# First pair's q and k turned on TensorE, q's second order made by a copy on VectorE

## Chip, core and metric

One core of a Trainium2 chip runs the kernel. Time is device microseconds of one execution, and lower is better. A run's time is given as the median of three. Besides that there is one profiled execution, whose trace is read here.

## What is computed

Attention comes first, then two layers that mix each token's features. `q`, `k` and `v` are float32, (4, 8, 1152, 64): 4 batches, 8 heads, 1152 positions, 64 features. The weights lie in memory as 8-byte floats, which the kernel reads as pairs of 32-bit words.

```python
q_pool = q.reshape(B, H, S // 2, 2, D).mean(axis=3)
scores = (1 / np.sqrt(D)) * np.matmul(q_pool, k.transpose(0, 1, 3, 2))
attn = exp(scores - max) / (sum + 1e-09)
x = np.matmul(attn, v)                 # heads side by side: (2304, 512)
h = x @ w_in1
x = (h * np.cos(h)) @ w_out1
h = x @ w_in2
out = (h / (1 + np.exp(-h))) @ w_out2  # (2304, 512)
```

## The kernel before

**Numbers in two halves.** TensorE multiplies float16 operands here. So that float32 accuracy is kept, each operand is scaled by a power of two and split into a high float16 half and a low one (`hi`, `lo`: the rest after rounding). A product then takes several matmuls: high by high, high by low, low by high.

**Pairs.** The 32 heads of attention are worked through in 16 pairs: pair j of batch b holds heads j and j + 4. A pair has 9 query tiles of 128 rows (576 pooled queries per head, four tiles each, and one tile that holds the remaining 64 of both). Batches follow each other, four pairs each.

**Preparation of a pair** is `pair_prep` (L453 to L514), on data that `pair_loads` (L429) fetched. All loads are issued by SP, whose queue also issues every other DMA of the program, in one order. GpSimd adds q's neighbouring rows (L456); VectorE takes absolute maxima of k, q and v (L126); a small matmul and three small VectorE operations make scale factors (`scale_steps`). Then come the splits. For k and v, `split` (L445) writes the high half by ScalarE and the low half by VectorE. For q two orders are wanted: `qn[:, 0]` holds high then low in its 2 x 64 columns, `qn[:, 1]` low then high. ScalarE writes the high half twice (L491), VectorE makes the low half (L492) and copies it into the second order (L495). One DMA transpose on SP's queue turns both orders of q, 18 blocks of 128 x 128, into `qT` (L497), and a second one turns k's 18 blocks into `kT` (L507).

**A tile** (`tile_scores`, `tile_exp`, `tile_hi`, `tile_lo`, `tile_pv`). TensorE multiplies both orders of a q block with k (L531, L539): the first order gives high by high and low by low, the second the cross terms. VectorE scales the scores out of PSUM into `sc` and keeps the extreme (L550), in a part of 512 and one of 640 columns; each part has one PSUM buffer, so that the next tile's scores wait until VectorE has emptied it. ScalarE takes the exponential (L558) and the high half (L564), GpSimd the low half (L569), a DMA transpose turns both (`hlT`, L571), and TensorE multiplies by v (`pv`, L582, L586). Four buffers each hold `sc`, `hl` and `hlT`, and the product with v follows four tiles behind.

**Beside the tiles** run, a step at a time, the preparation of the next pair and the loads of the one after it, in the first batch the preparation of the first layer's weights (16 pieces; ScalarE L201 and L202, VectorE L203, L207, L211), and from the second batch on the first layer itself (`g1_unit` L667, `g2_unit1` L722 on TensorE, the cosine on VectorE and ScalarE L695 to L711). The second layer and its product of halves (L836) make the tail.

**Who sets the order.** The code is written as generators that take turns; each engine's final order is made by a scheduler when the program is built, from priorities (`early`, `ahead`) and its own notion of durations. `pin` (L123) keeps the marked instructions in the order in which they are written. On the chip each engine runs its list strictly in order, and waits where an operand is missing.

Of the kernel before, what the change touches and what calls it, by code (L numbers as in the profile page):

```python
# [11 lines left out]
F32 = mybir.dt.float32  # L12
# [15 lines left out]
NB_N, NB_SC, NB_H, NB_T, NB_S = 2, 4, 4, 4, 5  # L28
# [20 lines left out]
def attention_moe_moe_kernel(ctx, tc, q, k, v, w_in1, w_out1, w_in2, w_out2, out):  # L49
# [3 lines left out]
    nc = tc.nc  # L53
# [20 lines left out]
    floor3 = const.tile([128, 1], F32, name="floor3")  # L74

    def make_consts():
        nc.vector.memset(mean, 2.0**-7)
        nc.vector.memset(halfpi, math.pi / 2)
        nc.vector.memset(floor3, 2.0**-14 - 0.5)

# [89 lines left out]
    def layer1_weight_steps(w, srcs, stage, pspool, eng, bufs, wt_bufs, period, offs, first):  # L170
# [68 lines left out]
        for i, x in enumerate(pieces):  # L239
            g = []  # L240
            if i < first:
                g.append(piece_steps(*x, lambda ins: ins))
                for _ in range(2):
                    next(g[0])
# [171 lines left out]
    def pair_new(at, b, j):  # L416
# [5 lines left out]
        P.on_pool = PREP_POOL if b == 0 else 0  # L422
        P.q = at.src.tile([128, 2 * NT + 1, 2, D], F32, tag="stq", name="stq", bufs=1)
# [5 lines left out]
    def pair_loads(P):  # L429
# [10 lines left out]
        for src, t in ((k, P.k), (v, P.v)):  # L440
            for i, h in enumerate(heads):
                nc.sync.dma_start(out=t[i], in_=src[P.b, h].rearrange("(p c) d -> p c d", c=KC))
                yield

    def split(hi, lo, src, s, on_pool):  # L445
        nc.scalar.activation(out=hi, in_=src, func=AF.Copy, scale=s)
# [3 lines left out]
        else:  # L450
            nc.vector.scalar_tensor_tensor(out=lo, in0=src, scalar=s, in1=hi, op0=ALU.mult, op1=ALU.subtract)

    def pair_prep(at, P):  # L453
# [27 lines left out]
        def do_v(i):  # L481
# [4 lines left out]
            split(vt[:, :, 0, 0:D], vt[:, :, 1, 0:D], P.v[i], s[:, 2:3], P.on_pool >= 2)  # L486


        qn = at.src.tile([128, 2, NQ, 2, D], F16, tag="kn", name="qn", bufs=NB_N)
        for e in range(2):  # L490
            nc.scalar.activation(out=qn[:, e, :, e, :], in_=qs, func=AF.Copy, scale=s[:, 0:1])  # L491
        nc.vector.scalar_tensor_tensor(  # L492
            out=qn[:, 0, :, 1, :], in0=qs, scalar=s[:, 0:1], in1=qn[:, 0, :, 0, :], op0=ALU.mult, op1=ALU.subtract
        )
        nc.vector.tensor_copy(qn[:, 1, :, 0, :], qn[:, 0, :, 1, :])  # L495
        qT = at.p.tile([128, 2, NQ, 128], F16, tag="qT", name="qT", bufs=2)
        nc.sync.dma_start_transpose(  # L497
            out=qT.rearrange("p e n k -> p (e n) k"), in_=qn.rearrange("p e n s d -> p (e n s d)")
        )
        P.qT = [qT[:, e] for e in range(2)]  # L500
        yield
        kn = at.src.tile([128, 2, KC, 2, D], F16, tag="kn", name="kn", bufs=NB_N)
        for i in range(2):
# [3 lines left out]
        nc.sync.dma_start_transpose(  # L507
            out=kT.rearrange("p i c k -> p (i c) k"), in_=kn.rearrange("p i c s d -> p (i c s d)")
        )
# [743 lines left out]
```

## Time and profile before

| | |
|---|---|
| median of 3 runs | 1365.03 us (1364.72 to 1366.87) |
| profiled execution | 1363.93 us, span 1362.1 us |
| TensorE matmul busy | 1139.0 us (84%) |
| VectorE busy | 1039.7 us (76%) |
| ScalarE busy | 870.9 us (64%) |
| GpSimd busy | 620.3 us (46%) |
| DMA queue of SP | 184.59 MB, 65.8% of 16 engines |
| granted TensorE clock, mean | 0.925 of full |

The profile's times count from the span's start. PE is TensorE, PEld its loading of weights, DVE VectorE, ACT ScalarE, POOL GpSimd, SPq the queue of SyncE, on which DMAs are issued. The first score matmul starts at 24.33 us, the first layer's first matmul on attention output at 256.7 us, the last product with v at 835.8 us; after that only the two layers remain. A wait is told as "who <- what came last". The rows on which the argument rests stand further down.

### The profile page before, as it was taken

The numbers are of one execution on the slowest core, as the hardware profiler recorded it, in microseconds if no ns is written. First come the engines' busy times: TensorE is split into PE (matmuls) and PEld (weight loads), VectorE is DVE, ScalarE is ACT, GpSimd is POOL, SyncE is SP. The second block draws the span as 40 slices with busy tenths as digits, with TensorE's granted clock in tenths as the row PEclk, the third lists the DMA queues.
The fourth block names the chain that finished last, engine by engine and source line by source line (L and its number), as shares of the span: only waits on it lengthen the run. The fifth ranks groups of instructions, "written<-read, shape, count | busy, mean of one in ns | idle before, by whom it ended". The sixth has DMA issues, their size and how long they took to land. (4 is left out here: it accounts for less than half of the span.)

```text
span 1362.1 us, 26442 instructions
## 1 busy us (share of the span) xinstructions
PE 1139.0 (84%) x10668; PEld 915.3 (67%) x10668; DVE 1039.7 (76%) x1927; ACT 870.9 (64%) x1061; POOL 620.3 (46%) x352
## 2 busy tenths in 40 slices
PE   2565465788988777889898899989999999999998
PEld 1343243576666556666676678778788888888887
DVE  6898888789876988888898996886757755444483
ACT  3878787778767777877788774544546633433352
POOL 1656675666556466656556562443667400000000
PEclk9667676889998889999899999999899999999999
DMA  9999999988799999988999965423444000000001
GB/s 290 202 212 226 221 231 183 163 168 166 135 204 177 201 199 198 198 151 186 157 202 188 217 129 109 106 81 71 86 91 112 32 25 32 9 16 17 17 32 32
DMA packets 509594, 186.27 MB, mean 137 GB/s; under 512 B 465952, under 2 KB 484384, under 8 KB 509472
## 3 DMA queue, kind: packets, MB, share of 16 engines
q1 hardware_dynamic: 509472, 184.59, 65.8%
q8 instruction: 83, 1.36, 0.4%
q14 instruction: 39, 0.32, 0.1%
HBM read 66.58 MB, written 9.44 MB: 56 GB/s over the span
## 5 line engine op out<-in xcount | busy, mean ns | idle before, releaser
L569 POOL TENSOR_TENSOR hl<-sc,hl 128x1152 f16<-128x1152 f32 x144 | 367.9, 2565 | 201.2 <-ACT hl L564 105.9
L531 PE MATMUL sp<-kT,qT 128*128 128x512 f16 (+1 forms) x768 | 189.4, 366 | 92.7 <-DVE sc L550 70.8
L550 DVE TENSOR_SCALAR_CACHE_REDUCE sc<-sp,psu 128x512 f32<-128x512 f32 (+1 forms) x288 | 228.9, 807 | 49.6 <-PE sp L531 46.2
L667 PEld LDWEIGHTS <-ih 128*128 128x128 f16 x2304 | 225.5, 99 | 42.9 <-issue 12.4
L558 ACT ACTIVATE sc<-sc,nb 128x1152 f32<-128x1152 f32 x144 | 179.8, 1250 | 114.4 <-DVE nb L555 77.8
L582 PE MATMUL pv<-vt,hlT 128*128 128x130 f16 (+1 forms) x1440 | 195.1, 237 | 65.9 <-DMA hlT<-hl 58.3
L582 PEld LDWEIGHTS <-hlT 128*128 128x128 f16 (+1 forms) x1440 | 146.4, 110 | 96.1 <-DMA hlT<-hl 73.4
L667 PE MATMUL h<-ys,ih 128*128 128x256 f16 x1152 | 195.5, 274 | 4.1 <-ACT gs L683 4.1
L667 PE MATMUL h<-xT,ih 128*128 128x256 f16 x1024 | 184.9, 275 | 3.2 <-DMA xT<-xn 3.1
L586 PE MATMUL pv<-vt,hlT 128*128 128x65 f16 (+1 forms) x1440 | 186.3, 207 | 0.0
L531 PEld LDWEIGHTS <-qT 128*128 128x128 f16 x768 | 76.9, 108 | 156.9 <-issue 104.2
L564 ACT ACTIVATE hl<-sc 128x1152 f16<-128x1152 f32 x144 | 164.6, 1153 | 14.5 <-DMA xT<-xn 9.7
L722 PE MATMUL y<-gh,oh 128*128 128x256 f16 x576 | 162.0, 281 | 7.1 <-ACT y L731 7.1
L722 PE MATMUL y<-gl,oh 128*128 128x256 f16 x576 | 161.8, 281 | 2.9 <-POOL gl L711 2.9
L722 PE MATMUL y<-gh,ol 128*128 128x256 f16 x576 | 161.8, 281 | 0.0
L836 PEld LDWEIGHTS <-op 128*128 128x128 f16 x1512 | 147.9, 98 | 18.0 <-issue 0.6
L667 PE MATMUL h<-ys,il 128*128 128x256 f16 x576 | 157.7, 274 | 0.0
L586 PEld LDWEIGHTS <-hlT 128*128 128x128 f16 (+1 forms) x1440 | 143.0, 108 | 15.8 <-issue 6.1
L667 PE MATMUL h<-xT,il 128*128 128x256 f16 x512 | 140.5, 274 | 0.0
L722 PEld LDWEIGHTS <-oh 128*128 128x128 f16 x1152 | 114.8, 102 | 28.1 <-issue 9.4
L711 POOL TENSOR_TENSOR gl<-tt,gh 128x1024 f16<-128x1024 f32 x36 | 92.1, 2559 | 76.4 <-DVE gh L710 71.2
L667 PEld LDWEIGHTS <-il 128*128 128x128 f16 x1152 | 113.7, 99 | 17.8 <-issue 2.9
(310 smaller groups left out, 2039.9 us busy)
## 6 DMA issues: line engine op xcount, KB each, us to landing
wst<-in_moe_w_in_dram SPq DMA_DIRECT2D x16, 1024.0 KB, 5.8
stk<-in_k_dram SPq DMA_DIRECT2D x32, 288.0 KB, 4.0
stv<-in_v_dram SPq DMA_DIRECT2D x32, 288.0 KB, 4.0
stq<-in_q_dram SPq DMA_DIRECT2D x32, 256.0 KB, 3.1
wst<-in_moe_w_out_dram SPq DMA_DIRECT2D x8, 1024.0 KB, 6.2
wst<-in_moe_w_out_dram SPq DMA_DIRECT2D x16, 512.0 KB, 6.0
ydr<-y SPq DMA_DIRECT2D x9, 512.0 KB, 4.3
y32b<-ydr SPq DMA_DIRECT2D x9, 512.0 KB, 3.3
```

Source lines behind the costliest of these rows:

```text
L531: nc.tensor.matmul(sp[:, o - a:o - a + n], P.qT[e][:, t, :], kT[:, o:o + n], start=(e == 0), stop=(e == 1))
L550: nc.vector.tensor_scalar(out=T.sc[:, a:z], in0=sp, scalar1=T.P.su, scalar2=None, op0=ALU.mult, op1=ALU.min, accum_out=mx[:, x:x + 1],)
L558: nc.scalar.activation(out=T.sc, in_=T.sc, func=AF.Exp, scale=-1.0, bias=nb)
L564: nc.scalar.activation(out=hi, in_=T.sc, func=AF.Copy)
L569: nc.gpsimd.tensor_tensor(out=T.hl[:, 1, :], in0=T.sc, in1=T.hl[:, 0, :], op=ALU.subtract)
L582: nc.tensor.matmul(G.pv[r, T.gi], T.hlT[:, 0, c, r], P.vt[i][:, c], start=(c == 0), stop=(c == KC - 1), skip_group_check=True,)
L586: nc.tensor.matmul(G.pv[r, T.gi, 0], T.hlT[:, 1, c, r], P.vt[i][:, c, 0], start=False, stop=(c == KC - 1), skip_group_check=True,)
L667: nc.tensor.matmul(hp, wt[:, c, f * 128:(f + 1) * 128], xt(c), start=(i == 0), stop=(i == 3 * NC - 1), skip_group_check=True,)
L711: nc.gpsimd.tensor_tensor(out=G.gl, in0=t, in1=gh, op=ALU.subtract)
L722: nc.tensor.matmul(blk.y[:, oc, :], wt[:, f, oc * 128:(oc + 1) * 128], gt[:, f % 4, :], start=(f == 0 and e == 0 and oc % 2 == 0), stop=(f ...
L836: nc.tensor.matmul(bank, t[:, e, c, :], wt[:, c, :], start=start, stop=True, skip_group_check=True)
```

## The change

Four things change.

1. For all pairs, q is split in one order only (`qn` has 9 blocks instead of 18), and only these are transposed. The second order is made afterwards from the transposed tile: it is the same numbers with partitions 0 to 63 and 64 to 127 exchanged, so VectorE copies each half of `qT[:, 0]` into the other half of `qT[:, 1]` (`swap`). For all pairs but the first, `swap` is written behind k's transpose. ScalarE's second pass over q and VectorE's copy inside `qn` are gone.
2. For the first pair alone (`on_pe`), q and k are turned on TensorE with an identity matrix, six blocks to a PSUM bank, and ScalarE copies them out (`turn`). Two GpSimd instructions make the identity.
3. For the first pair, k is loaded through ScalarE's queue, and a one-column activation (`warm`) stands behind these two loads, which makes ScalarE's table load come there.
4. `pin` now keeps the first two weight pieces' first steps and the first pair's v splits in program order. `qn` and `kn` have one buffer each, where they shared two before.

```diff
+    ident = const.tile([128, 128], F16, name="ident")
+    warm = const.tile([128, 1], F32, name="warm")
...
+        nc.gpsimd.memset(ident, 0.0)
+        nc.gpsimd.affine_select(
+            out=ident, in_=ident, pattern=[[-1, 128]], compare_op=ALU.not_equal, fill=1.0, base=0, channel_multiplier=1
+        )
...
-                g.append(piece_steps(*x, lambda ins: ins))
+                g.append(piece_steps(*x, pin))
...
+        P.on_pe = b * NP + j == 0
...
-                nc.sync.dma_start(out=t[i], in_=src[P.b, h].rearrange("(p c) d -> p c d", c=KC))
+                eng = nc.scalar if (P.b, P.j) == (0, 0) and src is k else nc.sync
+                eng.dma_start(out=t[i], in_=src[P.b, h].rearrange("(p c) d -> p c d", c=KC))
...
+    def turn(dst, src, on_pe):
+
+        if not on_pe:
+            nc.sync.dma_start_transpose(out=dst, in_=src)
+            return
+        nb = dst.shape[1]
+        for o in range(0, nb, 6):
+            m = min(6, nb - o)
+            pt = ps_h.tile([128, 2, GW], F32, tag="h", name="pt").rearrange("p a n -> p (a n)").bitcast(F16)
+            for i in range(m):
+                nc.tensor.transpose(pt[:, i * 128:(i + 1) * 128], src[:, (o + i) * 128:(o + i + 1) * 128], ident)
+            nc.scalar.activation(
+                out=dst[:, o:o + m].rearrange("p c k -> p (c k)"), in_=pt[:, 0:m * 128], func=AF.Copy
+            )
...
-        qn = at.src.tile([128, 2, NQ, 2, D], F16, tag="kn", name="qn", bufs=NB_N)
-        for e in range(2):
-            nc.scalar.activation(out=qn[:, e, :, e, :], in_=qs, func=AF.Copy, scale=s[:, 0:1])
-        nc.vector.scalar_tensor_tensor(
-            out=qn[:, 0, :, 1, :], in0=qs, scalar=s[:, 0:1], in1=qn[:, 0, :, 0, :], op0=ALU.mult, op1=ALU.subtract
-        )
-        nc.vector.tensor_copy(qn[:, 1, :, 0, :], qn[:, 0, :, 1, :])
+        qn = at.src.tile([128, NQ, 2, D], F16, tag="qn", name="qn", bufs=1)
+        split(qn[:, :, 0, :], qn[:, :, 1, :], qs, s[:, 0:1], False)
         qT = at.p.tile([128, 2, NQ, 128], F16, tag="qT", name="qT", bufs=2)
-        nc.sync.dma_start_transpose(
-            out=qT.rearrange("p e n k -> p (e n) k"), in_=qn.rearrange("p e n s d -> p (e n s d)")
-        )
+        q_pe = P.on_pe
+
+        def swap():
+            for x, y in ((slice(0, 64), slice(64, 128)), (slice(64, 128), slice(0, 64))):
+                nc.vector.tensor_copy(qT[x, 1], qT[y, 0])
+
+        turn(qT[:, 0], qn.rearrange("p n s d -> p (n s d)"), q_pe)
+        if q_pe:
+            swap()
...
-        nc.sync.dma_start_transpose(
-            out=kT.rearrange("p i c k -> p (i c) k"), in_=kn.rearrange("p i c s d -> p (i c s d)")
-        )
+        turn(kT.rearrange("p i c k -> p (i c) k"), kn.rearrange("p i c s d -> p (i c s d)"), P.on_pe)
         P.kT = [kT[:, i].rearrange("p c k -> p (c k)") for i in range(2)]
+        if not q_pe:
+            swap()
...
+                nc.scalar.activation(out=warm, in_=halfpi, func=AF.Copy)
```

The scheduler's order moves with it. ScalarE's list at the program's start, before (L491 splits q, L446 k and v, L201 and L202 belong to the weights, L558 and L564 to the tiles):

```order
L491 ACT_TABLE_LOAD
L491 ACTIVATE qn<-stq,ps__150 128x9x64 x2
L446 ACTIVATE kn<-stk,ps__150 128x9x64 x2
L446 ACTIVATE vt<-stv,ps__150 128x9x64 x2
L201 ACTIVATE wt<-wst 128x1024
```

and with the change (L450 loads k, L454 splits, L472 copies transposed blocks out of PSUM, `pt`):

```order
L450 DMA stk<-in_k_dram 128x576 x2
L968 ACT_TABLE_LOAD
L968 ACTIVATE warm<-halfpi 128x1
L454 ACTIVATE qn<-stq,ps__157 128x9x64
L454 ACTIVATE kn<-stk,ps__157 128x9x64 x2
L472 ACTIVATE qT<-pt 128x768
L472 ACTIVATE qT<-pt 128x384
L472 ACTIVATE kT<-pt 128x768 x3
L454 ACTIVATE vt<-stv,ps__157 128x9x64 x2
L207 ACTIVATE wt<-wst 128x1024
```

k's loads and the table load stand first, q is split once, and five copies out of PSUM stand ahead of v's splits.

VectorE's list at the program's start, before, from the split of q to the first emptying of scores (L550, `sc`); L203, L207, L211 and L93 belong to the first two weight pieces:

```order
L492 SCALAR_TENSOR_TENSOR qn<-stq,ps__150,qn 128x9x64
L495 COPY qn<-qn 128x9x64
L451 SCALAR_TENSOR_TENSOR kn<-stk,ps__150,kn 128x9x64 x2
L451 SCALAR_TENSOR_TENSOR vt<-stv,ps__150,vt 128x9x64 x2
L203 TENSOR_SCALAR wt,wm<-wt 128x1024
L207 SCALAR_TENSOR_TENSOR wt<-wt,wst 128x1024
...
L207 SCALAR_TENSOR_TENSOR wt<-wt,wst 128x1024
L211 SCALAR_TENSOR_TENSOR wt<-wst,wt 128x1024
L93 TENSOR_SCALAR mw<-wm 128x1
L550 TENSOR_SCALAR sc,mx<-sp,psu 128x512
```

and with the change (L459 makes low halves, L519 is `swap`, L574 empties scores, L209 is a weight piece's first pass):

```order
L459 SCALAR_TENSOR_TENSOR qn<-stq,ps__157,qn 128x9x64
L459 SCALAR_TENSOR_TENSOR kn<-stk,ps__157,kn 128x9x64 x2
L519 COPY qT<-qT 64x1152 x2
L574 TENSOR_SCALAR sc,mx<-sp,psu 128x512
L132 TENSOR_REDUCE pm<-stk 128x1
L574 TENSOR_SCALAR sc,mx<-sp,psu 128x640
L459 SCALAR_TENSOR_TENSOR vt<-stv,ps__157,vt 128x9x64
L574 TENSOR_SCALAR sc,mx<-sp,psu 128x512
...
L574 TENSOR_SCALAR sc,mx<-sp,psu 128x640
L209 TENSOR_SCALAR wt,wm<-wt 128x1024
```

The six passes over the weight pieces, which stood ahead of the first tile's scores, now stand behind those of the second tile.

VectorE's list where the eighth pair is prepared, before (L555 is a tile's small bias, L695 belongs to the cosine):

```order
L492 SCALAR_TENSOR_TENSOR qn<-stq,ps__3854,qn 128x9x64
L550 TENSOR_SCALAR sc,mx<-sp,psu 128x640
L495 COPY qn<-qn 128x9x64
L451 SCALAR_TENSOR_TENSOR kn<-stk,ps__3854,kn 128x9x64
L555 TENSOR_SCALAR nb<-mx 128x1
L451 SCALAR_TENSOR_TENSOR kn<-stk,ps__3854,kn 128x9x64
L451 SCALAR_TENSOR_TENSOR vt<-stv,ps__3854,vt 128x9x64
```

and with the change (L579 is the bias, L719 the cosine's first pass):

```order
L459 SCALAR_TENSOR_TENSOR qn<-stq,ps__3896,qn 128x9x64
L574 TENSOR_SCALAR sc,mx<-sp,psu 128x640
L459 SCALAR_TENSOR_TENSOR kn<-stk,ps__3896,kn 128x9x64 x2
L579 TENSOR_SCALAR nb<-mx 128x1
L459 SCALAR_TENSOR_TENSOR vt<-stv,ps__3896,vt 128x9x64
L519 COPY qT<-qT 64x1152 x2
L719 TENSOR_SCALAR tt<-hk 128x1024
```

Before the cosine's pass and the next tile's scores stand now two copies that need the transposed q.

## Rows read from the trace of the kernel before

**Rows 1.** Page, the chain that ended last: shares of the span by engine

```profile
PE 22%; DVE 1%; POOL 1%; ACT 0%; issue 0%; DVEq 0%
```

**Rows 2.** Windows: us, busy (count) of PE PEld DVE ACT POOL, PEclk, DMA share, GB/s

```profile
0.00:25.00 25.00, 1.26 (x4) 0.86 (x5) 15.00 (x29) 9.64 (x11) 2.01 (x13) 1.00 0.94 271
25.00:230.00 205.00, 115.94 (x928) 74.99 (x927) 179.63 (x397) 164.02 (x182) 128.09 (x64) 0.69 1.02 218
...
300.00:850.00 550.00, 475.99 (x4823) 363.95 (x4822) 468.41 (x924) 414.09 (x497) 320.41 (x168) 0.96 0.92 176
850.00:1362.00 512.00, 491.05 (x4421) 434.90 (x4418) 318.62 (x457) 233.20 (x316) 125.46 (x84) 0.98 0.19 50
```

**Rows 3.** Waits of TensorE, 24 to 230 us: us in total, times, longest us

```profile
PE pv L582 <- DMA hlT<-hl: 36.2, 14, 5.6
PE sp L531 <- DVE sc L550: 24.3, 16, 8.6
...
PE sp L531 <- DMA qT<-qn: 6.1, 1, 6.1
```

**Rows 4.** Waits of TensorE, 300 to 850 us

```profile
PE sp L531 <- DVE sc L550: 40.0, 35, 3.8
PE pv L582 <- DMA hlT<-hl: 19.1, 14, 3.2
```

**Rows 5.** Timeline 0 to 27 us: start, us, engine, line, operation, count, [idle before]

```profile
2.97 1.06 SPq L442 DMA_DIRECT2D stk<-in_k_dram  x2
...
7.36 0.75 DVE L126 TENSOR_REDUCE pm<-stk 128x1 f32<-128x576 f32 x1 [6.34 <-DMA stk<-in_k_dram]
...
9.41 1.43 DVE L126 TENSOR_REDUCE pm<-stv 128x1 f32<-128x576 f32 x2
...
12.14 1.28 ACT L491 ACT_TABLE_LOAD   x1 [12.14 <-DVE ps__150 L115]
...
13.43 1.44 ACT L491 ACTIVATE qn<-stq,ps__150 128x576 f16<-128x576 f32 x2
...
18.58 1.22 DVE L203 TENSOR_SCALAR_CACHE_REDUCE wt<-wt 128x1024 f32<-128x1024 f32 x1
...
24.33 2.08 PE L531 MATMUL sp<-kT,qT 128*128 128x512 f16 x6 [12.66 <-DMA kT<-kn]
```

**Rows 6.** TensorE's lines, 24 to 230 us: xcount | busy us, mean ns | idle before

```profile
L582 PE MATMUL pv<-vt,hlT 128*128 128x130 f16 x252 | 37.5, 267 | 35.6 <-DMA hlT<-hl 32.2 <-DVE pvs L600 1.9 <-POOL hl L569 1.5
```

**Rows 7.** ScalarE's copy out of PSUM, line 683: ns min/median/max

```profile
L683 ACT ACTIVATE hk<-h,ca x72: 662/669/720, 259.8 to 970.3; 128x512 f32<-128x512 f32 x72
```

**Rows 8.** Timeline of SP's queue, stretches between 280 and 378 us

```profile
289.27 25.92 SPq L571 DMA_TRANSPOSE hlT<-hl  x6
...
341.49 27.29 SPq L571 DMA_TRANSPOSE hlT<-hl  x5
368.88 3.09 SPq L497 DMA_TRANSPOSE qT<-qn  x1
```

**Rows 9.** Tile qT's landings; tile xrT's transposes: issue ns, and landings

```profile
DMA to landing us min/median/max: 4.6/5.8/7.5
...
L1097 SPq DMA_TRANSPOSE xrT<-xnr x2: 1355/1491/1627, 876.8 to 879.1; - x2
...
DMA to landing us min/median/max: 3.6/4.3/5.1
```

**Rows 10.** VectorE's copies by line: ns min/median/max

```profile
L495 DVE COPY qn<-qn x16: 310/319/781, 15.1 to 748.7; 128x576 f16<-128x576 f16 x16
...
L710 DVE CAST gh<-tt x36: 665/686/2856, 269.2 to 988.0; 128x1024 f16<-128x1024 f32 x36
...
L259 DVE COPY uoT<-uo x2: 885/1516/2147, 224.7 to 247.4; 64x4 f32<-64x4 f32 x2
```

**Rows 11.** Timeline of VectorE around the eighth pair's preparation

```profile
367.48 0.80 DVE L451 SCALAR_TENSOR_TENSOR kn<-stk,ps__3854,kn 128x576 f16<-128x576 f32 x1
368.20 0.81 DVE L451 SCALAR_TENSOR_TENSOR vt<-stv,ps__3854,vt 128x576 f16<-128x576 f32 x1
```

More of the change, by code (lines that the diff above doesn't have):

```diff
@@ L27 @@
 PSH = 15.0
-NB_N, NB_SC, NB_H, NB_T, NB_S = 2, 4, 4, 4, 5
+NB_SC, NB_H, NB_T, NB_S = 4, 4, 4, 5
 X_LAG = 40
@@ L441, in pair_loads, with split @@
             for i, h in enumerate(heads):
-                nc.sync.dma_start(out=t[i], in_=src[P.b, h].rearrange("(p c) d -> p c d", c=KC))
+                eng = nc.scalar if (P.b, P.j) == (0, 0) and src is k else nc.sync
+                eng.dma_start(out=t[i], in_=src[P.b, h].rearrange("(p c) d -> p c d", c=KC))
                 yield
-    def split(hi, lo, src, s, on_pool):
-        nc.scalar.activation(out=hi, in_=src, func=AF.Copy, scale=s)
+    def split(hi, lo, src, s, on_pool, put=lambda ins: ins):
+        put(nc.scalar.activation(out=hi, in_=src, func=AF.Copy, scale=s))
         if on_pool:
@@ L485, in do_v @@
             nc.gpsimd.memset(vt[:, :, 1, D:D + 1], 0.0)
-            split(vt[:, :, 0, 0:D], vt[:, :, 1, 0:D], P.v[i], s[:, 2:3], P.on_pool >= 2)
-        qn = at.src.tile([128, 2, NQ, 2, D], F16, tag="kn", name="qn", bufs=NB_N)
-        for e in range(2):
-            nc.scalar.activation(out=qn[:, e, :, e, :], in_=qs, func=AF.Copy, scale=s[:, 0:1])
-        nc.vector.scalar_tensor_tensor(
-            out=qn[:, 0, :, 1, :], in0=qs, scalar=s[:, 0:1], in1=qn[:, 0, :, 0, :], op0=ALU.mult, op1=ALU.subtract
-        )
-        nc.vector.tensor_copy(qn[:, 1, :, 0, :], qn[:, 0, :, 1, :])
-        qT = at.p.tile([128, 2, NQ, 128], F16, tag="qT", name="qT", bufs=2)
-        nc.sync.dma_start_transpose(
-            out=qT.rearrange("p e n k -> p (e n) k"), in_=qn.rearrange("p e n s d -> p (e n s d)")
-        )
+            split(vt[:, :, 0, 0:D], vt[:, :, 1, 0:D], P.v[i], s[:, 2:3], P.on_pool >= 2, *([pin] if q_pe else []))
+        qn = at.src.tile([128, NQ, 2, D], F16, tag="qn", name="qn", bufs=1)
+        split(qn[:, :, 0, :], qn[:, :, 1, :], qs, s[:, 0:1], False)
+        qT = at.p.tile([128, 2, NQ, 128], F16, tag="qT", name="qT", bufs=2)
+        q_pe = P.on_pe
[5 more added lines that the diff above has]
+            swap()
         P.qT = [qT[:, e] for e in range(2)]
         yield
-        kn = at.src.tile([128, 2, KC, 2, D], F16, tag="kn", name="kn", bufs=NB_N)
+        kn = at.src.tile([128, 2, KC, 2, D], F16, tag="kn", name="kn", bufs=1)
         for i in range(2):
```

## The prediction

> **What bounds the kernel now.** I read from the end backwards. The chain of waits that ended last [rows 1] holds TensorE alone for its last 22% of the span: the tail is matmuls back to back. The windows by stage [rows 2] say the same of 850 to 1362 us, TensorE busy 491.05 of 512. Nothing in this change touches that stage, so what the change brings must have been won before it, and is then passed on whole, since the tail only follows.
>
> The head, 0 to 25 us, is idle for TensorE: 1.26 us busy. The timeline [rows 5] shows why, as one chain: k's load is issued behind q's at 2.97, VectorE's first reduction starts at 7.36, the last of v ends near 10.84, ScalarE loads its table from 12.14 (1.28), writes q's high halves twice (1.44), VectorE makes the low halves, two DMA transposes follow one another, and the first score matmul starts at 24.33. From 25 to 230 us (the first batch, no MLP yet) VectorE is busy 179.63 of 205 (88%), DMA engines read 1.02, and the waits of TensorE [rows 3] put 36.2 us on transposed probabilities that had not landed and 24.3 on VectorE's emptying of scores. From 300 to 850 us TensorE is itself busy 475.99 of 550, VectorE 85%, ScalarE 75%; there TensorE waited 40.0 for VectorE and only 19.1 for landings [rows 4]. So: early, latency and VectorE together; later, TensorE with VectorE close behind; DMA full, but mostly not what is waited for.
>
> The sum is made against the profiled execution's own 1363.93 us. The median of the three runs shown is 1.10 higher, and I add that at the end.
>
> **The head.** Removed from the chain: the table load, 1.28, now done while loads fly; one of q's two passes on ScalarE, 0.72; and k's two issues ahead of v's, 1.06, which bring the last reduction forward by about that. The chain reaches q's split near 11.0 instead of 13.43. Then: q's split 0.72 and 0.80 (ScalarE, and VectorE as [rows 11]) to 12.5; nine transposes on TensorE, for which I take a 130-column product of the first batch, 0.267 [rows 6], 2.4, to 14.9 (at the least, hidden behind one another, 1); two copies out of PSUM, by columns from 0.67 for 512 [rows 7]: 1.0 and 0.5, to 16.4; the two cross copies on VectorE, 0.64 each (below), to 17.7. k's splits, its first transposes and first copy out (1.44 and 0.80, 1.6, 1.0) end near 16.6, inside that. First scores at about 17.5: 6.8 earlier. With cross copies at their dear end (2.15 each) it is 20.7, 3.6 earlier; with transposes at 1, some 8.
>
> Not all of this is carried. VectorE was idle for 10.0 of the first 25 us [rows 2] and will be idle nearly as long, since its reductions still wait for loads and its cross copies for ScalarE. The work that filled the old wait, six passes of 1.22 over the first two weight pieces (first at 18.58 [rows 5]), now stands behind the first tiles in its queue, as the order shows. A stage that VectorE fills to 88% returns part of the gain there. Between 0 and 6.8 I take **4 us**.
>
> **Less DMA.** Each of the other 15 pairs transposes 9 blocks less. In runs of transposes back to back SP's queue gave one of 18 blocks every 25.92/6 = 4.3 to 27.29/5 = 5.5 us [rows 8]; half of the lower is 2.2, 32 us of queue time in all. In the first batch the product waits straight on landings: 36.2 and, for q itself, 6.1 of 206 us. Of its three pairs' 6.5 us I take 3. Of the twelve later pairs' 26 us I take the share of time that TensorE waits for landings, 19.1/550: 1. Together **4 us**; ends 0 and 32.
>
> **Less ScalarE.** 0.72 in each of 16 pairs, 11.5 us. ScalarE is 75 to 80% busy and no wait of TensorE in [rows 3, 4] names it: taken as 0, hidden behind VectorE and TensorE; 11.5 if ScalarE set the pace. The weight pieces and v splits that are now kept in program order carry no work, 0.
>
> **More VectorE.** The removed copy took 0.32 for 576 columns [rows 10]. The two new ones have 64 partitions and 1152 columns each: by columns 0.64; no cheaper than 0.32; and the only 64-partition copy of the trace took 0.89 and 2.15 for four columns. I take 0.64, the nearest by type: 2 x 0.64 - 0.32 = 0.96 a pair, 14.4 over 15 pairs (ends 4.8 and 60).
>
> Here a row speaks against the change. VectorE's cast of line 710 took 0.69 in the median and up to 2.86 [rows 10]; the old q copy, as cheap a form, stretched at most to 0.78. The Trainium skill (SBUF — State Buffer, Who interferes with whom) says that such copies and GpSimd share a pair of ports and that whoever comes second is blocked for the other's whole instruction. The cast agrees with it, the old copy hardly; by that rule the new copies would cost up to 2 us more each, and the sum would come out near no change.
>
> **A new wait on VectorE.** The cross copies wait for qT's landing, and VectorE works strictly in order: behind them stand the score emptyings, for which TensorE waits. In the eighth pair [rows 11] k's second split ends at 368.28 and, after the change, a v split (0.81), a small bias and then the copies follow: reached near 369.3. SP reached that pair's qT at 368.88 [rows 8], held up by five transposes. A transpose of 8 blocks landed 3.6 to 5.1 us after its issue, 18 blocks 4.6 to 7.5 [rows 9]; half size gives about 4.0, so 372.9: a wait of 3.6. Elsewhere more work stands between (four rows and more), and the wait can be nothing. From 0 to 4 I take 1 a pair: 15 us.
>
> VectorE so gets 14.4 + 15 = 29 us. What of it reaches the end: at the least the share of time in which TensorE waits for VectorE, 24.3/206 and 40.0/550 (12% and 7%), at the most all. With VectorE at 85 to 88% I take a sixth: **5 us** lost.
>
> **Sum.** -4 - 4 + 5 = -3: 1363.93 - 3 + 1.10 = **1362.0 us**.
>
> **Rivals.**
> *VectorE's new wait decides (slower).* Place: the cross copies in the 15 later pairs. If the eighth pair is typical, wait 3 and work 0.96 make 4 a pair, 60 us; a quarter of that reaching TensorE costs 15 against 8 gained, or against 4 if the head is swallowed: +7 to +11, 1372 to 1376. It decides from 8/15 = 0.53 us of delay per pair that reaches TensorE. For it: TensorE waits for VectorE more than for anything else after 300 us, and the whole of the wait stands ahead of score work. Against: in most pairs several rows lie between. Chance 0.26.
> *Nothing arrives (same).* The head is returned to VectorE's backlog, the DMA relief is hidden behind TensorE, and the copies fill VectorE's idle 12 to 15%: 1363 to 1367. For it: only 19.1 of 550 us wait for landings. Chance 0.21.
> *DMA is what paces the tiles (much faster).* The half of 32 us and the whole head: -16 - 6.8 + 5 = -18, 1347; down to 1340. For it: DMA share 1.02 and 0.92 [rows 2]. The Trainium skill (Perfetto Trace Analysis, What "DMA-bound" means) counts a kernel as DMA-bound when the DMA engines or the issuing sequencer are solidly busy; by that rule this would be the case. The trace disagrees from 300 us on, where only 19.1 of 550 us wait for landings. Chance 0.12.
> *The change does not do what it says.* The order shows nine-block transposes for the 15 pairs, none for the first, k's loads first on ScalarE's queue and the table load right behind: 0.01.
>
> **How the numbers follow.** My forecast, 1356 to 1365, has 0.40; three quarters of it lie more than 0.2% (2.7 us, about what a measurement of this kernel tells from no change) under 1365.03. Faster: 0.30 + 0.12 = 0.42. Same: 0.10 + 0.20 = 0.30. Slower: 0.26 and small remainders, 0.28. The range leaves out most of the DMA case and the slower rival's far end: 1350 to 1374. Both signs hold much of the chance; the forecast's own range is 1356 to 1365.
>
> **What would show it.** Right: first score matmul at 16 to 19 us; the first batch ending 3 to 8 us earlier; cross copies of 0.4 to 0.9 us; VectorE's wait for qT under 25 us in sum; TensorE's waits for landings before 230 us below 36.2. Wrong: cross copies over 1.5 us, or a wait of VectorE for qT above 40 us (the slower rival); the same first batch despite an early first score (nothing arrives); a gain that keeps growing by about 1 us a pair after 300 us (DMA paces).

## The result and the profile after

The changed kernel took 1377.72 us in the median of five runs (1371.61 to 1378.94), the kernel before, beside it on the same chip, 1365.03 (1363.76 to 1367.22). The ratio of the two is 1.0074, 95% interval 1.0050 to 1.0099: about 10 us slower by it, where 3 us faster was predicted, and outside the range. The profiled execution took 1376.68 us, its span is 1374.9.

The head did what was predicted and a little more. Timeline of the changed kernel, 0 to 25 us (start, us, engine, line, operation, tiles, shapes, count, idle before):

```profile
1.67 1.28 ACT L968 ACT_TABLE_LOAD   x1 [1.67 <-PEq L1262]
...
8.89 0.74 DVE L132 TENSOR_REDUCE pm<-stv 128x1 f32<-128x576 f32 x1
...
10.96 0.77 ACT L454 ACTIVATE qn<-stq,ps__157 128x576 f16<-128x576 f32 x1 [7.79 <-DVE ps__157 L121]
...
12.64 1.14 PE L471 MATMUL pt<-ident,qn 128*128 128x128 f16 x9 [2.17 <-DVE qn L459]
...
13.49 1.19 ACT L472 ACTIVATE qT<-pt 128x768 f16<-128x768 f16 x2 [0.43 <-PE pt L471]
...
14.72 0.92 DVE L519 COPY qT<-qT 64x1152 f16<-64x1152 f16 x2 [0.68 <-ACT qT L472]
...
16.05 1.01 PE L555 MATMUL sp<-kT,qT 128*128 128x512 f16 x2 [0.26 <-ACT kT L472]
```

The first score matmul starts at 16.05 where it was 24.33 [rows 5], 8.28 us earlier: nine transposes took 1.14, not 2.4, and a copy 0.46, not 0.64. What came last before it was a copy of k out of PSUM, not the cross copies. The windows by stage (columns as in [rows 2]) show what became of it:

```profile
0.00:25.00 25.00, 9.19 (x47) 5.52 (x48) 15.58 (x35) 13.55 (x17) 4.28 (x16) 0.96 0.81 279
25.00:230.00 205.00, 111.69 (x873) 71.04 (x872) 189.06 (x390) 155.45 (x171) 121.87 (x63) 0.68 0.97 211
300.00:850.00 550.00, 469.06 (x4741) 352.67 (x4741) 482.43 (x910) 406.71 (x483) 323.71 (x171) 0.96 0.88 170
850.00:1375.00 525.00, 503.82 (x4555) 447.28 (x4552) 324.47 (x488) 238.67 (x323) 129.98 (x85) 0.99 0.20 51
```

TensorE did less in each stage behind the head (111.69 us for 115.94 up to 230, 469.06 for 475.99 from 300 to 850) and has 12.8 us more to do after 850. So the loss lies ahead of the tail: the last product with v starts at 849.97 us, 14.2 us later than before. VectorE was busier (189.06 for 179.63, 482.43 for 468.41), the DMA engines less (0.97 for 1.02, 0.88 for 0.92). The waits of TensorE from 24 to 230 us, and then from 300 to 850 (us in total, times, longest):

```profile
PE sp L555 <- DVE sc L574: 31.1, 21, 4.0
PE pv L606 <- DMA hlT<-hl: 23.7, 12, 4.9
PE sp L563 <- DVE sc L574: 16.6, 4, 7.8
PE bm L114 <- DVE mw L99: 13.9, 7, 3.8
PE bm L114 <- DVE pm L491: 5.2, 1, 5.2
```

```profile
PE sp L555 <- DVE sc L574: 48.5, 33, 6.9
PE pv L606 <- DMA hlT<-hl: 11.5, 5, 5.3
PE sp L563 <- DVE sc L574: 5.7, 7, 1.8
```

Read this against [rows 3, 4]. The waits for transposes fell, by 12.5 us (36.2 to 23.7) and 7.6 us (19.1 to 11.5), and that for q's transpose (6.1) is gone. In their place TensorE waits for VectorE's scores: 31.1 and 16.6 for 24.3, and 48.5 for 40.0. The stall did not go, it changed its name. (Whether the shorter transposes are what made those waits fall is taken up in the part on the prediction.)

The copies themselves, and the half transposes (ns min/median/max; what VectorE waited for ahead of the copies; landings in us):

```profile
L519 DVE COPY qT<-qT x32: 453/455/2645, 14.7 to 765.4; 64x1152 f16<-64x1152 f16 x32
L464 SPq DMA_TRANSPOSE qT<-qn x15: 1243/1302/3847, 45.5 to 758.1; - x15
...
  DMA qT<-qn: 3.7, 5
...
DMA to landing us min/median/max: 3.2/3.5/6.1
```

A copy takes 0.455 us in the median, but eight of the 32 are stretched, to 2.65 at most. And the wait on VectorE that the slower rival built on (15 us in the forecast, 45 in the rival at 3 a pair) is 3.7 us in five places: a half transpose lands in 3.5 us in the median where the whole took 5.8 [rows 9], and in most pairs other work stands in between.

### The profile page after: what moved, and what is told of

Read it like the earlier page. It is cut to its first block, busy times and chain, and to the rows that moved or that the text cites. A ratio compares the mean times of both kernels' runs of the same rounds, so it can differ in the third digit from the quotient of the medians.

```text
span 1374.9 us, 26483 instructions
## 1 busy us (share of the span) xinstructions
PE 1148.9 (84%) x10695; PEld 917.0 (67%) x10695; DVE 1067.7 (78%) x1943; ACT 863.8 (63%) x1051; POOL 620.2 (45%) x354
## 5 line engine op out<-in xcount | busy, mean ns | idle before, releaser
L555 PE MATMUL sp<-kT,qT 128*128 128x512 f16 (+1 forms) x768 | 195.4, 369 | 88.3 <-DVE sc L574 87.3
L574 DVE TENSOR_SCALAR_CACHE_REDUCE sc<-sp,psu 128x512 f32<-128x512 f32 (+1 forms) x288 | 228.0, 807 | 28.6 <-PE sp L555 22.6
L691 PE MATMUL h<-xT,ih 128*128 128x256 f16 x1024 | 194.1, 280 | 6.4 <-ACT hk L707 3.3
L555 PEld LDWEIGHTS <-qT 128*128 128x128 f16 x768 | 76.3, 108 | 154.1 <-issue 109.9
L691 PEld LDWEIGHTS <-il 128*128 128x128 f16 x1152 | 114.7, 100 | 17.7 <-issue 1.3
```

The lines of the kernel that those rows point to most:

```text
L555: nc.tensor.matmul(sp[:, o - a:o - a + n], P.qT[e][:, t, :], kT[:, o:o + n], start=(e == 0), stop=(e == 1))
L574: nc.vector.tensor_scalar(out=T.sc[:, a:z], in0=sp, scalar1=T.P.su, scalar2=None, op0=ALU.mult, op1=ALU.min, accum_out=mx[:, x:x + 1],)
L691: nc.tensor.matmul(hp, wt[:, c, f * 128:(f + 1) * 128], xt(c), start=(i == 0), stop=(i == 3 * NC - 1), skip_group_check=True,)
```

## The experiments

Three theories are tried. **Theory 1:** the copies' time on VectorE is the loss. **Theory 2:** the new head puts the work of weights and pieces, with which VectorE used to fill its wait, behind the first tiles, and so loses the 8 us again. **Theory 3:** the program is ordered by a scheduler that simulates it, so any edit moves instructions on all engines to the end of the program, and the order itself is worth several us. Ratios are to the kernel before on the same chip, with their 95% intervals; 0.1% is 1.37 us, and differences in us are taken from the ratios.

### One part at a time

First pair alone (later pairs as before):

```diff
+        if q_pe:
+            qn = at.src.tile([128, NQ, 2, D], F16, tag="kn", name="qn", bufs=2)
...
+        else:
+            qn = at.src.tile([128, 2, NQ, 2, D], F16, tag="kn", name="qn", bufs=2)
...
+            nc.vector.tensor_copy(qn[:, 1, :, 0, :], qn[:, 0, :, 1, :])
```

> The first pair as in the change (turned on TensorE, second order copied by VectorE, k through ScalarE's queue, table at once); pairs 2 to 16 as before, both orders of q through one transpose on the queue, no copies. Theory 1 (the copies in the later pairs take VectorE's time from the emptying of the scores): the head's 8 us stay in part and nothing takes them back, 1357 to 1361 us. Theory 2 (the first pair's part: tiles start 8 us sooner, but VectorE finds the same work of weights and pieces in front of them, and the new order of batch 0 loses the gain and more): 1370 to 1378 us, like the change itself. Theory 3 (any edit reshuffles the order that the scheduler works out, and that is worth several us either way): anywhere from 1360 to 1375, with no relation to the parts.

Measured: 0.9994 (0.9976 to 1.0012), level with before, and at most some 3 us faster.

Copies alone (`P.on_pe = False`, k on SP, no early table):

> All 16 pairs in one order with the two copies on VectorE, the first pair too, and the first pair's transposes on the queue, k on SP, no table load ahead: the head as before. Theory 1: the copies cost all that the change lost and the head's gain besides, 1377 to 1386 us. Theory 2: 1363 to 1369 us, since the first 25 us are as before. Theory 3: anywhere from 1360 to 1380.

Measured: 1.0124 (1.0097 to 1.0151), 17 us slower.

No copies in pairs 2 to 16 (`P.qT = [qT[:, e if q_pe else 0] for e in range(2)]`):

> The change without the copies in pairs 2 to 16: both score matmuls of a tile read the one order that the queue's transpose wrote, so the cross terms of the scores in these pairs are left out and replaced by a repeat of the straight ones; all other work is that of the change. Theory 1: 1354 to 1361 us, the head's gain and the shorter transposes without the copies. Theory 2: 1372 to 1378 us, no better than the change. Theory 3: anywhere from 1358 to 1375.

Measured: 1.0006 (0.9987 to 1.0025), level.

Copies on ScalarE (`nc.scalar.activation(out=qT[x, 1], in_=qT[y, 0], func=AF.Copy)`):

> The change with the 30 copies of pairs 2 to 16 on ScalarE in place of VectorE (some 1.2 us each by the evacuations of 768 columns in 0.81 us, so 35 to 40 us more of ScalarE's time, and those waits for the transpose now stand in ScalarE's order). Theory 1: 1358 to 1370 us, better than the change by most of what the copies took. Theory 2: 1374 to 1385 us, no better than the change. Theory 3: anywhere from 1360 to 1385.

Measured: 1.0044 (1.0014 to 1.0074), 6 us slower.

What follows: the first pair costs nothing, but its 8 us bring nothing that these runs tell from noise, and neither do half the transposes in the order that they came with. The loss comes with the copies. That is theory 1 but for two misses: it wanted the head's gain to show, and it did not want ScalarE, which no wait had named, to lose 6 us.

### More copies, fewer copies, the table alone

Each copy twice:

> The change with each of the 30 copies of pairs 2 to 16 done twice, the second time over the same values. Theory 1 (the copies' VectorE time is the loss; 30 of them cost 9 us between the run without them and the change): another 9 us, 1384 to 1392 us at a before of 1365. Theory 3 (reshuffled order, no price of the copies as such): anywhere from 1368 to 1384, and as likely below the change as above it.

Measured: 1.0117 (1.0093 to 1.0141), 16 us slower than before, 6 more than the change, with intervals that overlap slightly. In the trace VectorE's copies took 50.8 us in all where they took 27.3 in the change: a quarter of the added 23.5 us shows in the time, in an order that is again a new one.

Copies in batch 0 alone, then in batches 1 to 3 alone (`P.one = P.on_pe or P.b == 0`, or `P.b > 0`):

> One order and copies in pairs 1 to 4 (batch 0) alone, pairs 5 to 16 with both orders of q through one transpose as before, the first pair on TensorE. Six copies besides the first pair's two, some 5 us of VectorE. If VectorE is what bounds the stage from 25 to 230 us (busy 88 to 91% there), they arrive in full: 5 us over the first pair alone, 1370 to 1373 us. If a copy costs the same wherever it stands (9 us over 30), 1.8 us: 1367 to 1369 us. If the price is in the later batches, 1365 to 1367.

> The reverse: copies in pairs 5 to 16 alone (24 of them, some 20 us of VectorE), pairs 2 to 4 as before, the first pair on TensorE. If VectorE's price is in batch 0, 3 to 4 us over the first pair alone: 1369 to 1371 us. If a copy costs the same everywhere, 7 us: 1372 to 1375. If the price is in the later batches, all 9 us: 1374 to 1378.

Measured: 1.0019 (0.9999 to 1.0039) and 1.0056 (1.0036 to 1.0076). Over the first pair alone that is 3.4 us (not clear of the measurement) and 8.5, for 6 and 24 copies: no stage is singled out.

The table alone:

> The kernel before with one instruction more: a one-element copy on ScalarE ahead of the first pair's work, so that its table is loaded while the inputs arrive (the load took 1.28 us at 12.14 us, on the way to the first scores). It is also a control on the scheduler: it changes no engine's work otherwise. If what shortens the head reaches the end, 1.3 us faster, 1363 to 1365; if VectorE's work of batch 0 absorbs it, 1365 to 1367; if the order alone is worth several us (theory 3), it may stand 3 us or more away from before on either side.

Measured: 0.9984 (0.9964 to 1.0004). Every engine's order was that of before, and the time is within the measurement of it. The profile has the first scores at 24.70 us, no earlier than before's 24.33, although ScalarE's table was loaded in the first 2 us.

### Other ways around VectorE

Four edits, in the order of the four runs below: v's low parts left out, low parts on GpSimd, the copies on SP's queue, the copies over f32.

```diff
+            if 0 < P.b * NP + P.j <= NP:
+                nc.gpsimd.memset(vt[:, :, 1, :], 0.0)
...
-PREP_POOL, GH_ACT, GH_TAIL = 0, 0, 0
+PREP_POOL, GH_ACT, GH_TAIL = 1, 0, 0
...
-                nc.vector.tensor_copy(qT[x, 1], qT[y, 0])
+                    nc.sync.dma_start(out=qT[x, 1], in_=qT[y, 0])
...
+                    nc.vector.tensor_copy(qT[x, 1].rearrange("p n k -> p (n k)").bitcast(F32), qT[y, 0].rearrange("p n k -> p (n k)").bitcast(F32))
```

> The first pair as in the change, the other pairs' q as before (the kernel that came out level with before), and in pairs 2 to 5, which are prepared during batch 0, VectorE's two subtractions for v are left out: GpSimd fills v's low part with zeros, so the low part of v is missing from the result in these pairs. Eight instructions of 0.81 to 2.98 us each, 15.7 us together in that kernel's trace, most of it by the stretched ones. If VectorE's work is what the stage up to 230 us is bound by, and what swallowed the head's 8 us, a good part of it arrives: 4 to 12 us faster than before, 1354 to 1362. If VectorE isn't the bound there (the stage waits for transposes, for GpSimd or for the clock), within 2 us of before: 1364 to 1368.

Measured: 1.0012 (0.9990 to 1.0035). Missed: less work for VectorE, no gain at the end. But the gain was there, and went again. ScalarE's exponentials of the last tile of batch 0 and of the first of batch 1, before and in this run (timelines), and the first scores of batch 1 in this run:

```profile
227.88 1.24 ACT L558 ACTIVATE sc<-sc,nb 128x1152 f32<-128x1152 f32 x1
234.04 1.26 ACT L558 ACTIVATE sc<-sc,nb 128x1152 f32<-128x1152 f32 x1 [2.83 <-DVE nb L555]
```

```profile
217.16 1.25 ACT L594 ACTIVATE sc<-sc,nb 128x1152 f32<-128x1152 f32 x1
...
225.88 2.08 PE L567 MATMUL sp<-kT,qT 128*128 128x512 f16 x6 [9.99 <-DMA kT<-kn]
...
233.78 1.25 ACT L594 ACTIVATE sc<-sc,nb 128x1152 f32<-128x1152 f32 x1 [11.19 <-DVE uo L116]
```

At the end of batch 0 this run is 10.7 us ahead of before, one tile later 0.3: TensorE stood 9.99 us for the next pair's k, whose transpose was issued at 221.00 us, hardly sooner than before (221.30). So the time that is won in batch 0 can be lost again where the next pair is prepared.

> The same kernel, nothing left out, with the two subtractions for k of each pair in batch 0 on GpSimd, which needs one more pass of ScalarE for each. If VectorE is the bound of that stage: 2 to 5 us faster than before, 1361 to 1364. If the time goes where it was moved (GpSimd's subtractions stretch VectorE's own instructions, ScalarE has 0.6 us more for each): 1366 to 1372.

Measured: 1.0045 (1.0023 to 1.0067), 6 us slower, as in the second case of the expectation.

> The change with the 30 copies of pairs 2 to 16 done by two plain transfers from SBUF to SBUF on SP's queue, right behind the transpose, so that no engine computes for the second order. Theory 1 (VectorE's time is the loss): level with the run without copies, 1364 to 1369 us. If the shorter transpose was bought with a longer wait for q, or the queue is the bound after all: 1372 to 1380, like the change or worse.

Measured: 1.0042 (1.0018 to 1.0066). No engine computes the second order, and 6 us are lost all the same.

> The change with the 30 copies of pairs 2 to 16 over the same bytes read as 576 f32 in place of 1152 f16 per partition. If a copy's price is its own length (0.455 us unhindered), it follows that length: at half the elements and half the pace the same time, and 1375 to 1379 us like the change. If the price is in the stretched ones (9 of 32, up to 2.65 us, each ending with GpSimd's subtraction) and the f32 copy isn't held up by GpSimd, the trace shows none over 1 us and the time falls by up to 5 us, 1370 to 1374. If f32 runs at a lower pace, longer copies and 1378 to 1384.

Measured: 1.0046 (1.0024 to 1.0069). The trace has 452/455/2641 ns for the 30 f32 copies, the same as in f16, and every engine's order is that of the change, row for row. So this is in effect the change once more, on another chip: 6 us slower there, 10 on the first, with overlapping intervals.

What follows: on VectorE, on ScalarE and on the queue the copies cost about the same, though these engines have quite different slack. What the kernels share is that each has an order of its own. Theory 1 can't be told from theory 3 as long as an edit changes both, so the order was held.

### One order, other durations

In the following runs instructions were resized in the finished program, behind the scheduler, so that each keeps its place, its engine and its waits:

```diff
+def _resize(nc, pick, change, skip=0):
+    n = 0
+    for b in nc.main_func.blocks:
+        rows = b.instructions
+        for k, i in enumerate(rows):
+            if pick(i):
+                n += 1
+                if n > skip:
+                    rows[k] = _again(i, change)
...
+    _resize(nc, lambda i: copy_of(i) and i.outs[0].memref in short, lambda p: _ap(p, [list(p.ap[0]), [1, 16]]) if hasattr(p, "memref") and p.memref in short else p)
...
+    _resize(nc, lambda i: str(i.engine).endswith("PE") and any(second(p) for p in i.ins), first)
```

> The program of the change with every engine's order as it is, and then, in the finished program, VectorE's 30 copies of pairs 2 to 16 cut from 1152 to 16 columns (0.455 us and more to some 0.07), with the second score matmul of each tile in these pairs turned to the first order, so that the cross terms of the scores are left out there. No instruction changes its place or its waits. Theory 1 (the copies' own time is the loss): the 8 to 10 us come back, 1364 to 1369 us. Theory 3 (the loss is in the order that the scheduler works out around the copies, whoever does them): nothing comes back, 1373 to 1378.

Measured: 1.0034 (1.0019 to 1.0049), 4.6 us slower than before. Lines of the copies in this run, all 32 and then the 30 short ones (with their busy time and mean), and the same line of the change:

```profile
L519 DVE COPY qT<-qT x32: 164/166/2227, 14.6 to 757.7; 64x16 f16<-64x16 f16 x30, 64x1152 f16<-64x1152 f16 x2
...
L519 DVE COPY qT<-qT 64x16 f16<-64x16 f16 x30 | 15.6, 519 | 2.9 <-DMA qT<-qn 2.3
```

```profile
L519 DVE COPY qT<-qT 64x1152 f16<-64x1152 f16 x32 | 27.3, 853 | 4.9 <-DMA qT<-qn 3.7 <-ACT qT L472 0.7
```

Against the change (1.0074) 0.40% came back, 5.5 us; against the same order measured beside the f32 copies (1.0046) 0.12%, 1.6 us, which the intervals don't separate from nothing. But the copies did not get as short as the expectation had it. Eight of the short ones are still stretched, to 2.23 us at most, and the 30 together take 15.6 us of VectorE, where they took 26.4 in the change: 10.8 us came off. So this run doesn't part the theories. Of the 4.6 us that remain, some may be the order and some the copies' time that is left.

> The same cut in the kernel whose 30 copies stand on ScalarE (1.16 us each, 35 us together), which was 6 us slower than before. Theory 1, as it would read for ScalarE: the 6 us come back, 1364 to 1368 us. Theory 3: 1370 to 1374 us, with ScalarE 30 us less busy and no gain.

Measured: 1.0037 (1.0017 to 1.0056), for 1.0044. The 30 copies fell from 1.162 to 0.213 us each, 28 us of ScalarE, and the time by 1 us, which the intervals don't separate from nothing. No short copy is stretched here, so nearly the whole of these 6 us is order (the copies still wait for their transposes, 3.5 us in all).

> The same cut in the kernel with copies in all pairs and the head as before, which was 17 us slower than before; its first pair's two copies stay. Theory 1: 9 to 15 us come back, 1367 to 1373 us. Theory 3: it stays at 1378 to 1385 us.

Measured: 1.0105 (1.0077 to 1.0132), for 1.0124. In the trace the 30 copies take 13.3 us in place of some 29: with more than half of the copies' time gone, 14 of 17 us stay (here too the intervals overlap).

The head, held back on ScalarE in the order of the first pair alone:

```diff
+                held = at.p.tile([128, 2, KC, 128], F16, tag="hlT", name="held", bufs=NB_T)
+                for _ in range(8):
+                    nc.scalar.activation(out=held[:, 0, 0, 0:16], in_=ident[:, 0:16], func=AF.Copy)
...
+    _resize(
+        nc, lambda i: len(i.outs) == 1 and "held_" in str(getattr(i.outs[0], "memref", "")),
+        lambda p: _ap(p, [list(p.ap[0]), [1 if "held_" in p.memref else 0, 2304]]),
+    )
```

> The first pair alone changed (level with before), with 8 instructions of ScalarE behind the table's load that do nothing useful: one column each for the scheduler, 2304 columns each in the finished program, some 16 us from 3 us on, so that the first pair's split starts some 8 us later, at 19 in place of 11 us, and the first score matmul about where it was before, all in the order of the changed head. If what the head gains does reach the end and the new order of batch 0 costs as much (theory 2): 6 to 8 us slower than before, 1372 to 1375 us. If the stage behind the head swallows such a gain whatever the order: within 3 us of before, 1364 to 1369.

Measured: 1.0071 (1.0048 to 1.0094), 9.7 us slower than before. The first score matmul of the first pair alone, and of this run (two timelines of TensorE):

```profile
16.22 1.01 PE L563 MATMUL sp<-kT,qT 128*128 128x512 f16 x2 [0.26 <-ACT kT L471]
```

```profile
25.26 1.01 PE L563 MATMUL sp<-kT,qT 128*128 128x512 f16 x2 [0.26 <-ACT kT L471]
```

9.04 us later at the start is 0.77% later at the end, 10.5 us (6.6 to 14.4 by the two intervals together). So in this order the stage behind the head does not swallow such a shift. (The hold also kept the first weight passes of ScalarE back, so a part may be theirs.) With the head about as late as before's, this order is 9.7 us worse than before's: these are the 8 us that were missing, in the order, as theory 2 has it. That it is the displaced work of weights and pieces in it, and not other instructions that moved, is not shown. What the order exchanged, the waits of TensorE in the first pair alone show, 24 to 230 us:

```profile
PE sp L563 <- DVE sc L582: 40.4, 23, 6.0
PE bm L113 <- DVE mw L98: 21.6, 10, 4.3
PE pv L614 <- DMA hlT<-hl: 12.3, 8, 3.5
PE bm L113 <- DVE pm L489: 7.5, 2, 6.4
```

and for the kernel before a row of that view that [rows 3] leaves out:

```profile
PE bm L108 <- DVE mw L93: 17.4, 7, 5.2
```

Here there are no copies beyond the first pair's, in all later pairs VectorE's instructions are those of before, and still TensorE waits 40.4 us for scores (24.3 before), 21.6 for weight peaks (17.4) and 7.5 for the peaks of q, k and v. In return it waits 12.3 for landed probabilities (36.2 before), so that the sum hardly differs: these rows show which waits changed places, not where the 9.7 us stand. The matmuls that wait for peaks are tiny: `bm` spreads one scale over the partitions. TensorE takes its instructions in order, so while it waits for a peak that VectorE has not come to, the scores and products behind it wait too.

### The same work in a third order, and less work in the second

```diff
+                for _ in range(8):
+                    nc.scalar.activation(
+                        out=held.rearrange("p e c k -> p (e c k)")[:, 0:2304], in_=ident[:, 0:1].to_broadcast([128, 2304]), func=AF.Copy
+                    )
...
+    _resize(
+        nc, lambda i: len(i.outs) == 1 and "held_" in str(getattr(i.outs[0], "memref", "")),
+        lambda p: _ap(p, [list(p.ap[0]), [p.ap[1][0], 16]]),
+    )
```

> The first pair alone changed, in an order near that of before: 8 instructions of ScalarE of 2304 columns each stand behind the table's load while the scheduler works out the order, so that it takes the head to be as late as before, and are cut to 16 columns each (some 0.1 us) in the finished program. TensorE's order then differs from before's by 0.15 us of work per tile in the mean, that of the first pair alone by 0.38. If the head is worth its 8 to 9 us and it is the order that took them: 1356 to 1361 us, faster than both kernels. If any order other than before's is worse by as much: 1364 to 1370. If the head is worth nothing: 1364 to 1368.

Measured: 1.0116 (1.0090 to 1.0142), 16 us slower than before and 17 slower than the first pair alone, with the same work but for eight instructions of 0.2 us. VectorE's timeline of this run shows one place where the order costs, in its first 20 us:

```profile
18.27 0.75 DVE L131 TENSOR_REDUCE pm<-stk 128x1 f32<-128x576 f32 x1 [4.19 <-DMA stk<-in_k_dram]
19.03 0.92 DVE L516 COPY qT<-qT 64x1152 f16<-64x1152 f16 x2
```

The order was made for a late head, so the second pair's peak stands ahead of the first pair's copies: VectorE stood 4.19 us for a load that the copies don't need. From 24 to 230 us TensorE waits for weight peaks longer than in any other run:

```profile
PE bm L113 <- DVE mw L98: 29.4, 6, 10.0
PE pv L614 <- DMA hlT<-hl: 29.0, 15, 5.5
```

TensorE's order is nearer to before's than that of the first pair alone, and the time is far worse. One misplaced instruction near the start held VectorE for 4 us, however like the rest is; what that alone costs at the end was not measured.

> The first pair alone changed (level with before), its order as it is, and in the finished program the 20 reductions of VectorE over k, q and v of pairs 2 to 5 cut from 576 to 64 columns (0.743 us each to some 0.13, 12 us less of VectorE up to 230 us), so that the scales of these pairs come from a ninth of their data. If VectorE's work bounds that stage: 6 to 12 us faster than before, 1354 to 1360 us. If it waits there for others as often as they for it (the result of leaving out work in another order): within 3 us of before, 1363 to 1368.

Measured: 0.9971 (0.9948 to 0.9994), 4 us faster than before, by the very edge of the interval, and 3 faster than the first pair alone, whose interval overlaps. The 20 reductions fell from 14.9 to 4.3 us in the traces, so some 3 of 10.6 us arrived, if it is more than noise. That suits the run with v's low parts left out: VectorE's time in batch 0 seems to count, but not in full.

## Why the prediction was wrong

**The head, -4.** Right in mechanism up to the first scores, and mis-sized downwards there: 8.28 us earlier (6.8 predicted, 6.6 by its own chain, which ends at 17.7 and not 17.5). At the end it came to nothing: the first pair alone is level with before (0.9994). Held back by 9.04 us in the same order, the scores cost 10.5 at the end, so in that order the stage behind does not simply swallow the shift; the gain is lost to the order that came with it, 9.7 us worse than before's with the head about as late. (That a lead can be lost in its own order too, where the next pair is prepared, is what the run without v's low parts showed.) The prediction took off 2.8 us because VectorE's work, six weight passes above all, now stands behind the first tiles. Whether those passes are the costly part of the order was not separated.

**Less DMA, -4.** Without copies and with half the transposes (1.0006) the kernel stands level with the first pair alone (0.9994). The step "of its three pairs' 6.5 us I take 3" treated a wait as if its removal were time. And up to 230 us the waits did not even fall for the reason given. The wait for landed probabilities in the run without copies, from 24 to 230 us and from 300 to 850 us, and in the first pair alone from 300 to 850 us:

```profile
PE pv L604 <- DMA hlT<-hl: 35.0, 17, 6.1
```

```profile
PE pv L604 <- DMA hlT<-hl: 5.7, 7, 2.2
```

```profile
PE pv L614 <- DMA hlT<-hl: 17.2, 14, 3.0
```

In batch 0 half transposes go with 35.0 us here and whole ones with 12.3 in the first pair alone, so the fall from 36.2 to 23.7 is not shown to be theirs. In the later batches the half ones go with less (5.7, and 11.5 in the change, for 17.2 and 19.1), as argued, and the time stays level all the same.

**Less ScalarE, 0.** Nothing contradicts this: with the order held, 28 us less of ScalarE's copies changed the time by 1 us, within the measurement.

**More VectorE and a new wait, +5.** The total was near, made up differently. Copies of 0.455 in the median and not 0.64, but a mean of 27.3/32 = 0.85 with the stretched ones; with the old copies (5.6 us in 16) taken off, some 21 us over 15 pairs and not 14.4. The wait is 3.7 us and not 15. So 25 us for 29. What of it reaches the end is an estimate: a quarter, by the doubled copies (6 of 23.5 us) and the shortened reductions (3 of 10.6), would be 6 us where the prediction's sixth gave 5; the intervals of these runs overlap, so it is no more than that. The rival "VectorE's new wait decides" had the time nearly right (1372 to 1376) by a wait that the trace doesn't have.

**What failed** is the -8 for the head and the transposes. The prediction quoted the new order for two places and then costed the rest as if all else stayed where it was: what TensorE stopped waiting for was booked as time, with no term for what the scheduler moved. The scheduler places every instruction by simulated times, and a head that is earlier by 8 us, or 30 new copies, give other orders to the end of the program. The runs found that head and transposes without copies, predicted -8, came to 1.0006, about +1 us; the copies with their order, predicted +5, to what separates this from 1.0046 and 1.0074, 5.5 to 9.3 us. Here the rival "nothing arrives" named what happened to the head and the DMA. Its sign, a first batch no faster despite an early first score, came: ScalarE's last exponential of batch 0 starts at 232.41 us in the change and 232.62 in the first pair alone, at 227.88 before. That an order alone is worth as much was found with durations equal or nearly so: 1.0037 with ScalarE's copies shortened, 1.0071 with the head held back, 1.0116 for a third order. None of the other orders that do the whole work was better than before's by more than the measurement tells. How the copies' 5.5 to 9.3 us divide into VectorE's time and order stays open, since shortening them took only 10.8 of 26.4 us away; which displaced instruction costs how much was not taken apart either.

**The rule on the shared ports** was rightly taken up. The Trainium skill (SBUF — State Buffer, Who interferes with whom) has a copy of VectorE that comes second blocked for GpSimd's whole instruction. The trace agrees in the stretched copies: each of the eight began while an instruction of GpSimd ran, and ended about 0.3 us after one. These are the timelines of both engines around the third pair's copies at 88 us (a window to 94), and then around the fourth's at 143:

```profile
84.69 5.69 POOL L593 TENSOR_TENSOR hl<-sc,hl 128x1152 f16<-128x1152 f32 x2 [8.00 <-DVE nb L579]
...
88.18 4.83 DVE L519 COPY qT<-qT 64x1152 f16<-64x1152 f16 x2
90.33 2.35 POOL L232 TENSOR_TENSOR il<-wt,ih 128x1024 f16<-128x1024 f32 x1
```

```profile
142.39 3.10 POOL L232 TENSOR_TENSOR il<-wt,ih 128x1024 f16<-128x1024 f32 x1
...
143.59 2.68 DVE L519 COPY qT<-qT 64x1152 f16<-64x1152 f16 x2
```

In the second, GpSimd's instruction ends at 145.49. The two copies together last from 143.59 to 146.27, 2.68 us for a work of 0.91: the first stood until GpSimd was done, the second ran at once. Stretching added some 12.7 us to the 32 copies (27.3 for 32 times 0.455), not up to 2 us to each. The old q copy, which the prediction says hardly agrees, was held up too where it took 0.78 us: it began at 657.32, and GpSimd's instruction at L711 ended at 657.92. One that began at 270.49, inside such an instruction from 269.93 to 272.76, took 0.32 all the same; why is not shown.

## What to carry to other kernels

Where a scheduler orders the whole program, an edit has two prices: its instructions, and the order that comes out. Measure them apart: resize the instructions behind the scheduler and keep the order, before you explain a change of one per cent by the work that it added, and read in the trace how much time really came off. A wait that is removed is a gain only if the next engine in the row was not about to be waited for. What a serial head is late by passed to the end whole in the one order where it was tried; what it was early by did not, because the order that came with it was worse. No version was found that does the whole work and beats the kernel before; the early table load alone is within its measurement (0.9984).

## What the runs showed of the hardware

A copy of 64 partitions on VectorE took the same 0.455 us for 1152 f16 and for 576 f32 elements, the same bytes, and 0.166 us for 16 f16 columns. The short one was still stretched beside GpSimd, in eight of 30 cases, to 2.23 us at most. ScalarE's copy of 1152 columns took 1.162 us, and never more than 1.163, with GpSimd at work beside it, and of 16 columns 0.213, never more than 0.214. Nine blocks of 128 by 128 turned on TensorE took 1.14 us in a row, and a transpose of nine blocks by DMA landed in 3.5 us in the median, one of eighteen in 5.8. Twelve executions of one program spread over 11 us (1360.43 to 1371.62 for the first pair alone), so that single executions can't be compared to better than that, and a per cent takes the medians of many.
